# Local attention and a feed-forward network on one core: PE visits attention for two units at a time

## The chip, the core and the metric

The kernel runs on one core of a Trainium2 chip. It is one program; the metric is the device time of one execution in microseconds (us), as the median of three runs. Engines: PE (TensorE, the matrix unit, with PEld for its weight loads), ACT (ScalarE), DVE (VectorE), POOL (GpSimd) and SP, which here only issues DMAs. Every engine works through its own instructions in the order in which the program lists them; semaphores tie the engines together.

## The reference

Attention with 4 batches, 8 heads, 768 positions and 64 values per head, where a position sees the first 8 keys and the last 96 ones, with a slope per head; then a feed-forward network of 512 x 2048 over the 3072 tokens.

```python
scores = scale * np.matmul(q, k.transpose(0, 1, 3, 2))
keep = is_global | is_local              # first 8 keys; 0 <= i - j < 96
scores = np.where(keep, scores - slopes * dist, -1e9)
a = np.exp(scores - np.max(scores, axis=-1, keepdims=True))
a = a / (np.sum(a, axis=-1, keepdims=True) + 1e-09)
x = np.matmul(a, v)                      # as (3072, 512)
h = x @ w_in                             # (3072, 2048)
return np.maximum(0.01 * h, h) @ w_out   # (3072, 512)
```

## The kernel before

Both halves run in one stream on PE. The feed-forward half is cut into 8 chunks of 384 tokens and 16 slices f of the hidden 2048, which makes 128 steps j. A step is `ffn1(j)`, 12 matmuls of 384 columns into `ps_h` (H(j) below), and then `ffn2(j - 1)`, 9 matmuls of 512 columns into the three `ps_o` tiles of the chunk. Three matmuls stand where one would do in plain arithmetic, since x, the weights and the hidden values g are each split into a high and a low part (`xh`, `xl`, `wih`, `wil`, `gh`, `gl`). Between the two products stands `hidden`: ACT copies `ps_h` to t (L717), DVE takes the leaky maximum in place (L718), ACT rounds it to gh (L723), DVE takes the rest gl (L724). `ps_h` has one buffer, so H(j + 1) waits for the copy of H(j). PSUM is full: `ps_o` has 3 banks, `ps_h` one, and `ps_x` four, two under the tag `ps_av` and two under `ps_t`.

The attention half is cut into 48 units: 24 blocks of 128 queries (6 per batch), each with its 8 heads in two halves. A unit sees 192 gathered keys, in the first block of a batch (units 0, 1, 12, 13, 24, 25, 36, 37) 128. Unit u takes three visits of PE, called events: `event(t)` computes attention times v for unit t - 2 and the scores of unit t into the same two banks; all are 64x64 matmuls, four of which share the array. Units from 14 on (`BY_DVE`) are not transposed by PE: `sums` scales the probabilities by the reciprocal of their sum, DVE transposes 32x32 blocks (L232), and `move` writes them to DRAM (`via`) and reads them back into `pt`. The tag `ps_t` served the transposes of units 0 to 13 alone.

Behind the matmuls of an event the order in the code is: ACT copies x of unit t - 2 out of PSUM (`keep_x`, L313); POOL splits it into xh and xl (`split_x`, L43 and L326; x has one buffer); DVE adds the biases of unit t and takes the largest values (`biased`, four L188, which wait for the copy of x); ACT takes four exponentials with their sums (`exps`, L201); DVE forms rs (L222, L223), scales (four L229) and transposes. From step 23 on these instructions are not pinned to the order of the code (`pin`): the framework's scheduler sorts them among the steps' t, gh and gl, when the program is built.

`ev_at` tells at which step an event stands: the six events of a chunk were spread over 14 of its 16 steps, two or three apart. x of a chunk must be whole when the steps of that chunk begin.

Of the kernel before, what the change touches and what calls it, by code (L numbers as in the profile page):

```python
# [10 lines left out]
F32 = mybir.dt.float32  # L11
# [7 lines left out]
P = 128  # L19
D = 64  # L20
NU = 2
BY_DVE = 14
TB = 32
G = 32
# [9 lines left out]
def spread(items, slots):  # L34

    out = {}
    for n, x in enumerate(items):
        out.setdefault(slots[n * len(slots) // len(items)], []).append(x)
    return out
# [7 lines left out]
def fast_path(ctx, tc, qp, kp, vp, wi, wo, nvec, weights, nmall, out, B, H, S):  # L47
# [4 lines left out]
    NF = wi.shape[0]  # L52
# [14 lines left out]
    ps_x = ctx.enter_context(tc.tile_pool(name="ps_x", bufs=1, space=bass.MemoryType.PSUM))  # L67
# [42 lines left out]
    units = {}  # L110
    NUNIT = NSTEP * NU
    LEAD = NU * CHUNKS[0]

# [12 lines left out]
    def head(u, pr, a, j):  # L126

        if u < BY_DVE:
            n = 2 * j + a
# [11 lines left out]
    def load_qk(u):  # L141
        s, uu, i = where(u)
        if uu == 0:
            qs[s] = raw.tile([P, 2 * NU, P], F32, tag="qkr", name="qs")
            nc.sync.dma_start(out=qs[s], in_=qp[s])
        k = raw.tile([P, 2, 2, KW], F32, name="kr")
        if i:
            nc.sync.dma_start(out=k, in_=kp[s, uu])
        elif u < BY_DVE:
            nc.sync.dma_start(out=k[:, :, :, HALF:], in_=kp[s, uu][:, :, :, HALF:])  # L150
        else:
            kd, ks = (x.rearrange("p a f (s x) -> p (a f s) x", s=2) for x in (k, kp[s, uu]))
            nc.sync.dma_start(out=kd[:, :, TB:], in_=ks[:, :, TB:])
        units[u] = dict(q=qs[s][:, 2 * uu:2 * uu + 2], k=k)

    def load_v(u):
        s, uu, i = where(u)
        v = raw.tile([P, 5, 2, D], F32, name="vr", bufs=3)
        g0 = 0 if i else 3
        nc.sync.dma_start(out=v[:, g0:], in_=vp[s, uu][:, g0:])  # L160
        units[u]["v"] = v

    def scores(u, av):
        d = units[u]
        s, uu, i = where(u)
        q, k = d.pop("q"), d.pop("k")


        for a in range(2):
            for f in range(2):  # L170
                qf = slice(f * HALF, (f + 1) * HALF)
                for j in range(2):
                    rows = slice(j * D, (j + 1) * D)
                    tc.keep_in_program_order(nc.tensor.matmul(  # L174
                        own(u, av[qf, j, a * KW:(a + 1) * KW]), lhsT=q[rows, a, qf], rhs=own(u, k[rows, a, f, :]),
                        start=True, stop=True))

    def biased(u, ps):
        d = units[u]
        s, uu, i = where(u)  # L180
        pr = att.tile([P, 4 * KW], F32, name="pr")
        nm = nmall[:, 4 * u:4 * u + 4]
        for a in range(2):
            for j in range(2):
                nb = (nbw if i else nb0)[:, 4 * uu + 2 * a + j, :]
                if u >= BY_DVE:
                    nb = nb.rearrange("p (s x) -> p s x", s=2)
                pin(nc.vector.tensor_tensor_reduce(  # L188
                    out=head(u, pr, a, j), in0=own(u, ps[:, j, a * KW:(a + 1) * KW]), in1=nb, scale=-0.125, scalar=3.0e38,
                    op0=ALU.add, op1=ALU.min, accum_out=nm[:, 2 * a + j:2 * a + j + 1]))  # L190
        d.update(pr=pr, nm=nm)
# [92 lines left out]
    def attn_v(u, av):  # L284
        d = units[u]
        s, uu, i = where(u)
        v, pt = d["v"], d["pt"]

        def near(rows, j, g, f):

            if u < BY_DVE:
                return pt[rows, 3 * j + g] if f is None else pt[rows, 3 * j + g, f]
            n = g if where(u)[2] else g - 1
            return blocks(u, pt)[rows, slice(0, 4) if f is None else slice(2 * f, 2 * f + 2), j, n * TB:(n + 1) * TB]

        for j in range(2):
            for a in range(2):
                rows, out = slice(a * HALF, (a + 1) * HALF), slice(j * D, (j + 1) * D)
                tc.keep_in_program_order(nc.tensor.matmul(av[out, a, 2 * KW:], lhsT=v[rows, 4, j, :], rhs=near(rows, j, 2, None),  # L299
                                 start=True, stop=False))  # L300
        for f in range(0 if i else 1, 2):
            for g in range(0 if i else 1, 2):
                for j in range(2):
                    for a in range(2):
                        rows, out = slice(a * HALF, (a + 1) * HALF), slice(j * D, (j + 1) * D)
                        tc.keep_in_program_order(nc.tensor.matmul(av[out, a, 2 * KW + f * HALF:2 * KW + (f + 1) * HALF],  # L306
                                         lhsT=v[rows, 2 * f + g, j, :], rhs=near(rows, j, g, f),
                                         start=False, stop=(f == 1 and g == 1)))

    def keep_x(u, av):  # L310
        d = units[u]
        x = att.tile([P, 2, P], F32, name="x", bufs=1)
        pin(nc.scalar.copy(out=x, in_=av[:, :, 2 * KW:]))  # L313
        d["x"] = x

    def split_x(u):
        x = units.pop(u)["x"]
        s, uu, i = where(u)
        c = max(c for c in range(NCHUNK) if first_step[c] <= s)
        si = s - first_step[c]  # L320
        if c not in xt:
            xt[c] = [xts.tile([P, NK, CT], F32R, tag="xt", name=name) for name in ("xh", "xl")]
        cols = slice(si * P, (si + 1) * P)
        xh, xl = xt[c][0][:, 2 * uu:2 * uu + 2, cols], xt[c][1][:, 2 * uu:2 * uu + 2, cols]
        pin(copy_exact(nc.gpsimd, xh, x))
        pin(nc.gpsimd.tensor_tensor(out=xl, in0=x, in1=xh.bitcast(F32), op=ALU.subtract))  # L326

    def event(t, conv=()):

        now, mid, old = t < NUNIT, t - 1 in units, t - 2 in units  # L330
        if t < LEAD + 2:

            av = (ps_lead if t % 2 else ps_x).tile([P, 2, 512], F32, tag="ps_av", name="ps_sc")
            scores(t, av)
            if mid:
                transposes(t - 1)
            if old:
                ov = ps_lead.tile([P, 2, 512], F32, tag="ps_ov", name="ps_ov")
                attn_v(t - 2, ov)
        else:  # L340

            ov = av = ps_x.tile([P, 2, 512], F32, tag="ps_av", name="ps_av")
            attn_v(t - 2, ov)
            if now:
                scores(t, av)
            if mid:
                transposes(t - 1)
            keep_x(t - 2, ov)
        if t + 2 < NUNIT:
            load_qk(t + 2)  # L350
        if t + 1 < NUNIT:
            load_v(t + 1)
        if t < STAGES - 3:
            load_piece(t + 2)
        ends = due[:]
        due.clear()
        if ends:
            ends[0]()
        scale, shift, low = conversion(conv[0]) if conv else [lambda: None] * 3
        scale()  # L360
        if now:
            biased(t, av)
            exps(t)
        if ends:
            ends[1]()
        shift()
        if now:
            sums(t)
        low()
        if mid:  # L370
            keep_pt(t - 1)
        if old and t < LEAD + 2:
            keep_x(t - 2, ov)
        if old:
            split_x(t - 2)


    half = 7
    order = ([(0, f) for f in range(half)] + [(1, f) for f in range(NF)] + [(0, f) for f in range(half, NF)]
# [44 lines left out]
    for c in range(1, NCHUNK):  # L424
        events = range(NU * first_step[c] + 2, NU * first_step[c + 1] + 2)
        slots = (range(0, half - 1) if c == 1 else [23, 25, 26, 28, 29, 31] if c == 2 else [33, 35, 37, 40, 42, 44] if c == 3
                 else range((c - 1) * NF, c * NF - 2))
        ev_at.update(spread(events, slots))

    for t in range(2):  # L430
# [13 lines left out]
    for j in range(len(order) + 1):  # L444
        pinned[0] = j < half + NF
        conv = list(conv_at.get(j, ()))
        for t in ev_at.get(j, ()):
            event(t, conv[:1])
            conv = conv[1:]

        def end():
            for step in due:
                step()
            due.clear()

        def more():
            for n, p in enumerate(conv):
                if n:
                    end()
                for step in conversion(p):  # L460
                    step()
        if j == half:

            scale_bias(tc, tabs[:, 1], nbw, H, 2)
            scale_bias(tc, tabs[:, 0, HALF:], nb0, H, 2)
        if j < len(order):
            ffn1(j, end, more)
        if j:
            ffn2(j - 1)
# [342 lines left out]
```

## Time and profile before

| what | us |
|---|---|
| runs | 663.36, 663.47, 665.22 (median 663.47) |
| profiled execution, its own time | 663.89 |
| its span, first to last instruction | 662.0 |
| PE busy | 629.2 |
| DVE busy | 360.3 |
| ACT busy | 284.1 |
| POOL busy | 81.1 |

The span is what the profile's page divides; the execution's own time is 1.9 us longer. Busy times are unions of an engine's instructions. In the rows of the views below, a row is an engine, a line of the kernel, the operation, what it writes from what it reads, and how many; in the timeline it begins with the start and the length in us and ends, in brackets, with the engine's idle time before it and the instruction that ended it.

### The profile page before, as it was taken

Reading aid. Unit: us, or ns where it says so; the run is one execution under the profiler, and the core shown is the slowest. Engines: PE = TensorE matmul, PEld = TensorE weight load, DVE = VectorE, ACT = ScalarE, POOL = GpSimd, SP = SyncE. Lnnn points to the kernel's source line nnn. Section 1 sums busy time; section 2 is a strip of 40 time slices with the busy share of each in tenths; the row PEclk is TensorE's granted clock in tenths of the full one; section 3 lists DMA queues with packets and bytes.
Section 4 is the critical chain, followed back from the end, with each engine's and each line's share of the span. In section 5 each row is a group of like instructions: output and inputs, shape, how many; then the busy total and the mean of one; then the engine's idle time right before and its main releaser. Section 6 shows DMA issues by size and latency. Waiting matters only on the chain.

```text
span 662.0 us, 14799 instructions
## 1 busy us (share of the span) xinstructions
PE 629.2 (95%) x5803; PEld 552.0 (83%) x5803; DVE 360.3 (54%) x1073; ACT 284.1 (43%) x796; POOL 81.1 (12%) x146
## 2 busy tenths in 40 slices
PE   4669989999999999999999999999999999999994
PEld 3558879898888888888888888988888888999993
DVE  4968988887566545464544545355453644222221
ACT  5877755454444343353434343353342433232221
POOL 3344610000111010010100101010100011000000
PEclk9889999999999999999999999999999999999998
DMA  8785634332665543254441543245442431010001
GB/s 315 250 322 185 215 120 142 127 96 76 216 212 193 192 119 120 96 191 149 151 154 62 188 125 120 84 147 169 135 173 61 171 92 49 1 48 1 1 0 53
DMA packets 55166, 88.09 MB, mean 133 GB/s; under 512 B 9776, under 2 KB 30256, under 8 KB 55088
## 3 DMA queue, kind: packets, MB, share of 16 engines
q1 hardware_dynamic: 55088, 87.06, 39.9%
q8 instruction: 48, 0.79, 0.5%
q14 instruction: 30, 0.25, 0.1%
HBM read 67.90 MB, written 19.14 MB: 131 GB/s over the span
## 4 chain that ended last, share of the span: by engine, by line
PE 89%; DVE 3%; ACT 3%; DMA 2%; issue 1%; SPq 0%; POOL 0%; ACTq 0%; POOLq 0%; DVEq 0%
PE ps_h L713 14%; PE ps_h L714 13%; PE ps_h L715 13%; PE ps_o L736 13%; PE ps_o L734 13%; PE ps_o L735 13%; PE ps_av L174 4%; PE ps_av L306 3%; PE ps_av L299 2%; DMA kr<-in_kp_dram 2%; PE ps_tr L260 1%; ACT pr L201 1%; DVE w L489 1%; DVE w L493 1%; ACT w L484 0%
## 5 line engine op out<-in xcount | busy, mean ns | idle before, releaser
L713 PE MATMUL ps_h<-xh,wih 128*128 128x384 f32 x512 | 177.1, 346 | 0.0
L714 PE MATMUL ps_h<-xl,wih 128*128 128x384 f32 x512 | 172.3, 337 | 0.0
L715 PE MATMUL ps_h<-xh,wil 128*128 128x384 f32 x512 | 172.3, 336 | 0.0
L734 PE MATMUL ps_o<-woh,gh 128*128 128x512 f32 x384 | 150.2, 391 | 2.6 <-ACT kept L403 1.7
L736 PE MATMUL ps_o<-woh,gl 128*128 128x512 f32 x384 | 151.7, 395 | 0.1
L735 PE MATMUL ps_o<-wol,gh 128*128 128x512 f32 x384 | 150.5, 392 | 0.0
L718 DVE SCALAR_TENSOR_TENSOR t<-t 128x384 f32<-128x384 f32 x128 | 73.1, 571 | 137.8 <-ACT t L717 137.7
L717 ACT COPY t<-ps_h 128x384 f32<-128x384 f32 x128 | 60.6, 473 | 191.1 <-PE ps_h L715 191.1
L713 PEld LDWEIGHTS ps_h<-xh,wih 128*128 128x128 f32 x512 | 96.6, 189 | 13.4 <-issue 8.8
L714 PEld LDWEIGHTS ps_h<-xl,wih 128*128 128x128 f32 x512 | 96.6, 189 | 3.6
L715 PEld LDWEIGHTS ps_h<-xh,wil 128*128 128x128 f32 x512 | 96.5, 188 | 0.0
L724 DVE TENSOR_TENSOR gl<-t,gh 128x384 fp32r<-128x384 f32 x128 | 73.8, 576 | 40.6 <-ACT gh L723 40.6
L723 ACT CAST gh<-t 128x384 fp32r<-128x384 f32 x128 | 65.7, 513 | 66.8 <-DVE t L718 65.0
L201 ACT ACTIVATE pr<-pr,nmall 128x192 f32<-128x192 f32 (+1 forms) x192 | 83.4, 436 | 18.5 <-DVE nmall L188 18.0
L736 PEld LDWEIGHTS ps_o<-woh,gl 128*128 128x128 f32 x384 | 72.1, 188 | 16.8 <-DVE gl L724 1.6
L734 PEld LDWEIGHTS ps_o<-woh,gh 128*128 128x128 f32 x384 | 72.1, 188 | 14.4 <-ACT kept L403 2.1
L735 PEld LDWEIGHTS ps_o<-wol,gh 128*128 128x128 f32 x384 | 72.1, 188 | 11.1
L43 POOL TENSOR_SCALAR xh<-x 128x256 fp32r<-128x256 f32 x48 | 20.9, 435 | 435.4 <-ACT x L313 362.1
L188 DVE CUSTOM_DVE_ANT_0 pr<-ps_av,nbw 128x192 f32<-128x192 f32 x136 | 40.5, 354 | 52.5 <-ACT x L313 52.5
L313 ACT COPY x<-ps_av 128x256 f32<-128x256 f32 x42 | 15.6, 373 | 73.3 <-PE ps_av L174 69.4
L326 POOL TENSOR_TENSOR xl<-x,xh 128x256 fp32r<-128x256 f32 x48 | 37.0, 772 | 4.0
L201 ACT ACTIVATION_READ_ACCUMULATOR pr<-pr,nmall 128x1 f32 x192 | 36.2, 188 | 0.0
(84 smaller groups left out, 485.1 us busy)
## 6 DMA issues: line engine op xcount, KB each, us to landing
kr<-in_kp_dram SPq DMA_DIRECT2D x40, 384.0 KB, 3.9
vr<-in_vp_dram SPq DMA_DIRECT2D x40, 320.0 KB, 3.3
via<-pr SPq DMA_DIRECT2D x30, 384.0 KB, 2.3
pt<-via SPq DMA_DIRECT2D x120, 96.0 KB, 2.3
wst<-in_wi_dram SPq DMA_DIRECT2D x16, 512.0 KB, 3.6
wst<-in_wo_dram SPq DMA_DIRECT2D x16, 512.0 KB, 3.6
qs<-in_qp_dram SPq DMA_DIRECT2D x24, 256.0 KB, 4.2
out_dram<-part SPq DMA_DIRECT2D x21, 256.0 KB, 2.1
```

The costliest lines, as they stand in the source:

```text
L188: pin(nc.vector.tensor_tensor_reduce(out=head(u, pr, a, j), in0=own(u, ps[:, j, a * KW:(a + 1) * KW]), in1=nb, scale=-0.125, scalar=3.0e38 ...
L201: pin(nc.scalar.activation(out=p, in_=p, func=AF.Exp, scale=-1.0, bias=nm[:, 2 * a + j:2 * a + j + 1], accum_out=sm[:, 2 * a + j:2 * a + j ...
L713: tc.keep_in_program_order(nc.tensor.matmul(ps, lhsT=wih[:, k, fs], rhs=xh[:, k, :CT], start=(k == 0), stop=False))
L714: tc.keep_in_program_order(nc.tensor.matmul(ps, lhsT=wih[:, k, fs], rhs=xl[:, k, :CT], start=False, stop=False))
L715: tc.keep_in_program_order(nc.tensor.matmul(ps, lhsT=wil[:, k, fs], rhs=xh[:, k, :CT], start=False, stop=(k == NK - 1)))
L717: pin(nc.scalar.copy(out=t, in_=ps))
L718: pin(nc.vector.scalar_tensor_tensor(out=t, in0=t, scalar=0.01, in1=t, op0=ALU.mult, op1=ALU.max))
L723: pin(nc.scalar.copy(out=gh, in_=t))
L724: pin(nc.vector.tensor_tensor(out=gl, in0=t, in1=gh.bitcast(F32), op=ALU.subtract))
L734: tc.keep_in_program_order(nc.tensor.matmul(o, lhsT=gh[:, ts_], rhs=woh[:, f, :], start=first, stop=False))
L735: tc.keep_in_program_order(nc.tensor.matmul(o, lhsT=gh[:, ts_], rhs=wol[:, f, :], start=False, stop=False))
L736: tc.keep_in_program_order(nc.tensor.matmul(o, lhsT=gl[:, ts_], rhs=woh[:, f, :], start=False, stop=last))
```

## The change

From unit 22 on `event(t)` is replaced by `visit(t, t + 1)`. It computes attention times v for the units t - 2 and t - 1, then the scores of t and t + 1, each unit in two banks of its own: the even one under `ps_av`, the odd one under `ps_t`. Then come the copies and splits of both x, the biases and exponentials of both, and the sums, transposes and moves of both. A chunk has three visits, in its steps 1, 6 and 11, in place of six events; in the chunk before the change of pace the events 20 and 21 and the visits 22 and 24 stand at the steps 0, 3, 7 and 12 of it.

```diff
+PAIRS = 22
+    def visit(*ts):
+        for t in ts:
+            if t - 2 in units:
+                avs[t] = ps_x.tile([P, 2, 512], F32, tag="ps_t" if t % 2 else "ps_av", name="ps_v")
+                attn_v(t - 2, avs[t])
+        for t in ts:
+            if t < NUNIT:
+                scores(t, avs[t])
+        for t in ts:
+            if t + 2 < NUNIT:
+                load_qk(t + 2)
+            if t + 1 < NUNIT:
+                load_v(t + 1)
+        for t in ts:
+            keep_x(t - 2, avs[t])
+            split_x(t - 2)
+        for t in ts:
+            if t < NUNIT:
+                biased(t, avs.pop(t))
+                exps(t)
+        for t in ts:
+            if t < NUNIT:
+                sums(t)
...
+        if c > 3:
+            events, slots = events[::2], [(c - 1) * NF + s for s in (1, 6, 11)]
+        elif c == 3:
+            events, slots = [20, 21, 22, 24], [2 * NF + s for s in (0, 3, 7, 12)]
...
-            event(t, conv[:1])
+            if t >= PAIRS:
+                visit(t, t + 1)
+            else:
+                event(t, conv[:1])
```

How the built program stands on three engines (rows in the order of the program; x4 is four in a row). Lines of the changed file lie 1 to 36 further down. PE at the unit 30, before:

```order
L736 MATMUL ps_o<-woh,gl 128x512
L299 MATMUL ps_av<-pt,vr 64x128 x4
L306 MATMUL ps_av<-pt,vr 64x64 x16
L174 MATMUL ps_av<-kr,qs 64x192 x8
L713 MATMUL ps_h<-xh,wih 128x384
L714 MATMUL ps_h<-xl,wih 128x384
```

and now:

```order
L772 MATMUL ps_o<-woh,gl 128x512
L300 MATMUL ps_v<-pt,vr 64x128 x4
L307 MATMUL ps_v<-pt,vr 64x64 x16
L300 MATMUL ps_v<-pt,vr 64x128 x4
L307 MATMUL ps_v<-pt,vr 64x64 x16
L175 MATMUL ps_v<-kr,qs 64x192 x16
L749 MATMUL ps_h<-xh,wih 128x384
```

The matmuls of unit 31, which stood two steps later, now stand between the same two matmuls of the feed-forward half. ACT at the same place, before:

```order
L313 COPY x<-ps_av 128x256
L201 ACTIVATE pr,sm<-pr,nmall 128x2x96 x4
L717 COPY t<-ps_h 128x384
L723 CAST gh<-t 128x384
L717 COPY t<-ps_h 128x384
```

and now, at the visit of 28 (five steps earlier, the rows up to the second gh) and at that of 30:

```order
L314 COPY x<-ps_v 128x256
L202 ACTIVATE pr,sm<-pr,nmall 128x2x96 x4
L314 COPY x<-ps_v 128x256
L202 ACTIVATE pr,sm<-pr,nmall 128x2x96
L753 COPY t<-ps_h 128x384
L202 ACTIVATE pr,sm<-pr,nmall 128x2x96 x3
L759 CAST gh<-t 128x384
L753 COPY t<-ps_h 128x384
```

```order
L314 COPY x<-ps_v 128x256
L202 ACTIVATE pr,sm<-pr,nmall 128x2x96 x4
L314 COPY x<-ps_v 128x256
L202 ACTIVATE pr,sm<-pr,nmall 128x2x96 x4
L753 COPY t<-ps_h 128x384
L759 CAST gh<-t 128x384
```

The copy of ps_h behind a visit now stands behind five exponentials or behind eight. The first form is found at the visits of 22, 26, 28, 32, 38, 40 and 44, the second at those of 24, 30, 34, 36, 42 and 46. DVE at unit 30, before (biases of the unit ahead of these rows):

```order
L222 TENSOR_SCALAR rs<-sm 128x4
L223 RECIPROCAL rs<-rs 128x4
L718 SCALAR_TENSOR_TENSOR t<-t 128x384
L229 TENSOR_SCALAR pr<-pr,rs 128x2x96 x4
L724 TENSOR_TENSOR gl<-t,gh 128x384
L232 STREAM_TRANSPOSE pr<-pr 128x768
```

and now (biases of unit 30 ahead of them; of the four biases of unit 31 the first is shown):

```order
L223 TENSOR_SCALAR rs<-sm 128x4
L224 RECIPROCAL rs<-rs 128x4
L230 TENSOR_SCALAR pr<-pr,rs 128x2x96 x4
L189 ISA pr,nmall<-ps_v,nbw 128x2x96
...
L233 STREAM_TRANSPOSE pr<-pr 128x768
L223 TENSOR_SCALAR rs<-sm 128x4
L224 RECIPROCAL rs<-rs 128x4
L230 TENSOR_SCALAR pr<-pr,rs 128x2x96 x4
L754 SCALAR_TENSOR_TENSOR t<-t 128x384
L233 STREAM_TRANSPOSE pr<-pr 128x768
L760 TENSOR_TENSOR gl<-t,gh 128x384
```

The scales of unit 30 moved ahead of the biases of unit 31, and the step's t behind the scales of both. At the visits of the first form the four biases stand straight behind the first reciprocal, and the scales behind them; at those of 24 and 36 as well, but there t stands behind both transposes.

More of the change, by code (lines that the diff above doesn't have):

```diff
@@ L375, in event @@
             split_x(t - 2)
+    def visit(*ts):
[21 more added lines that the diff above has]
+                sums(t)
+    avs = {}
     half = 7
```

## The prediction

> **What bounds the kernel now.** I read the page's head first, then the busy time of PE (TensorE) over the stretch that the change touches (columns: stretch, length, busy time, matmuls, granted clock, DMA share, GB/s).
>
> ```profile
> span 662.0 us, 14799 instructions
> PE 629.2 (95%) x5803; PEld 552.0 (83%) x5803; DVE 360.3 (54%) x1073; ACT 284.1 (43%) x796; POOL 81.1 (12%) x146
> 235.00:560.00 325.00, 325.00 (x2784) 1.00 0.40 129
> ```
>
> From 235 to 560 us PE has work in flight all the time at the full granted clock: this stretch costs what PE's instructions cost, and PE waits for nobody. So two questions decide: what PE pays less, and whether the others still keep up. PE's timeline, one step without a visit and one behind a visit (start, length, then the group):
>
> ```profile
> 310.56 0.34 PE L713 MATMUL ps_h<-xh,wih 128*128 128x384 f32 x1
> ...
> 312.64 0.39 PE L734 MATMUL ps_o<-woh,gh 128*128 128x512 f32 x1
> ...
> 314.48 0.40 PE L736 MATMUL ps_o<-woh,gl 128*128 128x512 f32 x1
> 314.80 0.45 PE L299 MATMUL ps_av<-pt,vr 64*64 64x128 f32 x8
> 315.07 0.64 PE L306 MATMUL ps_av<-pt,vr 64*64 64x64 f32 x32
> 315.54 0.83 PE L174 MATMUL ps_av<-kr,qs 64*64 64x192 f32 x16
> 316.30 0.44 PE L713 MATMUL ps_h<-xh,wih 128*128 128x384 f32 x1
> 316.58 0.34 PE L714 MATMUL ps_h<-xl,wih 128*128 128x384 f32 x1
> ...
> 320.55 0.34 PE L713 MATMUL ps_h<-xh,wih 128*128 128x384 f32 x1
> ```
>
> Narrower windows show where the second group of four starts inside L299 and inside L174:
>
> ```profile
> 314.96 0.29 PE L299 MATMUL ps_av<-pt,vr 64*64 64x128 f32 x4
> 315.70 0.67 PE L174 MATMUL ps_av<-kr,qs 64*64 64x192 f32 x12
> ```
>
> A bare step is 12 matmuls H(j) into ps_h in 2.08 us (0.173 each) and 9 into ps_o in 2.07 (0.23 each): 4.15. Around the visit four things cost more than streaming: from L736 to L299 0.32 in place of 0.23; the first group of four L299 0.16 where the second takes 0.11; the last L174 group, 0.76 for four groups where one takes 0.16; the first L713 0.28 in place of 0.17. Together 0.09 + 0.05 + 0.11 + 0.10 = 0.35 us a visit: the price of going into 64x64 tiles and back. [...]
>
> **What ACT, DVE and POOL do behind such a visit:**
>
> ```profile
> 316.49 0.37 ACT L313 COPY x<-ps_av 128x256 f32<-128x256 f32 x1 [1.98 <-PE ps_av L174]
> 317.30 0.46 ACT L201 ACTIVATE pr<-pr,nmall 128x192 f32<-128x192 f32 x1 [0.43 <-DVE nmall L188]
> ...
> 319.07 0.45 ACT L717 COPY t<-ps_h 128x384 f32<-128x384 f32 x1
> 320.15 0.52 ACT L723 CAST gh<-t 128x384 fp32r<-128x384 f32 x1 [0.62 <-DVE t L718]
> ```
>
> ```profile
> 316.89 0.36 DVE L188 CUSTOM_DVE_ANT_0 pr<-ps_av,nbw 128x192 f32<-128x192 f32 x1 [1.79 <-ACT x L313]
> ...
> 318.01 0.08 DVE L188 DVE_READ_ACCUMULATOR2_ANT nmall<- 128x1 f32 x1
> 319.19 0.17 DVE L222 TENSOR_SCALAR rs<-sm 128x4 f32<-128x4 f32 x1 [1.10 <-ACT pr L201]
> ...
> 319.56 0.56 DVE L718 SCALAR_TENSOR_TENSOR t<-t 128x384 f32<-128x384 f32 x1
> 320.03 1.00 DVE L229 TENSOR_SCALAR pr<-pr,rs 128x192 f32<-128x192 f32 x4
> 320.94 0.56 DVE L724 TENSOR_TENSOR gl<-t,gh 128x384 fp32r<-128x384 f32 x1
> 321.41 0.97 DVE L232 STREAM_TRANSPOSE pr<-pr 128x768 f32<-128x768 f32 x1
> ```
>
> ```profile
> 316.95 0.41 POOL L43 TENSOR_SCALAR xh<-x 128x256 fp32r<-128x256 f32 x1 [12.88 <-ACT x L313]
> 317.44 0.74 POOL L326 TENSOR_TENSOR xl<-x,xh 128x256 fp32r<-128x256 f32 x1
> ```
>
> I count from the start of H(j) behind the visit, 316.30. The copy of ps_h, t(j), stands on ACT behind the four exponentials: 2.77 to 3.22. PE wants ps_h back at 4.25 (320.55; ps_h has one buffer): 1.03 us to spare. gh(j) ends at 4.37 and gl(j) at 5.20; the second product wants them at 4.25 + 2.08 = 6.33 and, its third matmul, at 6.79. This slack is the cover of the whole softmax, and a double visit puts twice the softmax in front of the same t(j).
>
> **The change, part by part.** Units 22 to 49 are 28 visits of one, and become 14 of two. PE's matmuls for them are the same, the second unit's follow in the same tiles. Gain: 14 x 0.35 = 4.9 us. Bounds: nothing, if the second unit starts as dearly as the first; 6.3, if its two L299 groups stream at the pace of L306 besides (0.47 for eight, 0.06 in place of 0.11: 0.10 less a visit). I take 4.9, since in the rows the dear start comes once, at the change of shape.
>
> The double visit on ACT: x(t), four exponentials, x(t+1), exponentials of t+1, and t(j) among or behind these. x(t) is free when the scores of t are done, which is 4 x 0.16 = 0.65 earlier against H(j): x(t) at 0.19 - 0.65 = -0.46, exponentials (0.81 later) 0.35 to 2.12 (319.07 - 317.30 = 1.77 for four), x(t+1) 2.12 to 2.49. POOL costs nothing here: it frees x 1.69 after x(t)'s start, at 1.23. DVE takes rs of t 0.12 after ACT's last exponential, at 2.24, and is free 0.37 later, 2.61. From here the two forms of the order part.
>
> *Biases of t+1 next (seven visits, beginning with units 22, 26, 28, 32, 38, 40, 44).* They start at 2.61, the first exponential 0.41 later at 3.02, then t(j) stands behind this one: 3.46 to 3.94. PE waits only past 4.2: spare 0.26, no stall. DVE: biases to 3.81, scales of t 0.91, t(j) 0.47, the transpose 0.95, rs 0.17, so gl(j) ends near 6.8 where it is wanted at 6.75: 0 to 0.2 us each; I take 0.06, together 0.4.
>
> *Scales of t first (units 30, 34, 42, 46).* Biases of t+1 start at 2.61 + 0.91 = 3.52, exponentials at 3.93, and t(j) stands behind all four: 5.70 to 6.18. What PE loses on top at a restart, an older wait shows:
>
> ```profile
> 166.59 0.58 ACT L416 COPY part<-ps_o 128x512 f32<-128x512 f32 x1
> ```
>
> ```profile
> 167.22 0.50 PE L734 MATMUL ps_o<-woh,gh 128*128 128x512 f32 x1 [0.65 <-ACT part L416]
> 167.55 0.39 PE L735 MATMUL ps_o<-wol,gh 128*128 128x512 f32 x1
> ```
>
> 0.05 after the copy's end, and 0.33 to the next matmul in place of 0.23: 0.10. So H(j+1) starts at 6.23 in place of 4.25: 1.98 + 0.10 = 2.1 us. Behind it rs of t+1 at 5.8, scales 6.2 to 7.1, t(j) to 7.7, gh(j) to 8.2 (wanted at 8.4), the transpose to 8.55, gl(j) to 9.05 (wanted at 8.85): 0.2 + 0.1. Sum 2.4 each, three times 7.2. In the visit of 46 the flag's seven small DVE instructions stand between as well:
>
> ```profile
> L585 DVE TENSOR_REDUCE fl<-nmall 128x1 f32<-128x192 f32 x1 | 0.4, 353 | 0.0
> ```
>
> They hold t(j) and gl(j) some 1.0 us longer (0.35 and six shorter ones): 3.3.
>
> *First blocks (units 24 and 36), whose scores have 128 columns:*
>
> ```profile
> 255.04 0.37 ACT L313 COPY x<-ps_av 128x256 f32<-128x256 f32 x1 [1.78 <-PE ps_av L174]
> 255.78 0.40 ACT L201 ACTIVATE pr<-pr,nmall 128x128 f32<-128x128 f32 x1 [0.37 <-DVE nmall L188]
> ...
> 257.35 0.46 ACT L717 COPY t<-ps_h 128x384 f32<-128x384 f32 x1
> ```
>
> ```profile
> 255.45 0.29 DVE L188 CUSTOM_DVE_ANT_0 pr<-ps_av,nb 128x128 f32<-128x128 f32 x1 [1.60 <-ACT x L313]
> ...
> 258.31 0.87 DVE L229 TENSOR_SCALAR pr<-pr,rs 128x128 f32<-128x128 f32 x4
> ...
> 259.56 0.71 DVE L232 STREAM_TRANSPOSE pr<-pr 128x512 f32<-128x512 f32 x1
> ```
>
> x(t) at 0.19 - 4 x 0.11 = -0.24; exponentials 0.50 to 2.07; biases of t+1 at 2.56, exponentials 2.89 to 4.46, t(j) to 4.94: H(j+1) at 4.99, 0.74 + 0.10. On DVE t(j) stands behind scales and transpose of both units, until about 6.7; gh(j) ends at 7.8, wanted at 7.15: 0.7 + 0.1. Sum 1.6 each, 3.2. The last visit, 48, has no scores and costs nothing.
>
> SP issues the same transfers; what is new is that the second unit's way through DRAM stands behind the first's four reads:
>
> ```profile
> 322.42 0.33 SPq L212 DMA_DIRECT2D via<-pr  x1
> pt<-via SPq DMA_DIRECT2D x120, 96.0 KB, 2.3
> ```
>
> First write near 6 (late form 9.9), reads 2.3 later for 1.8, second write and reads as long again, landing 2.3: near 17 (20.4). The next visit comes 5 or 6 steps on, at 20.8 at the earliest, and where the form is late PE is 2.4 later too. This costs nothing; with three steps it would.
>
> Sum: -4.9 + 0.4 + 7.2 + 3.3 + 3.2 = +9.2 us. The profiled execution took 663.89 us (span 662.0 and 1.9 around it), 0.42 above the median 663.47; from the first 673.1, from the median 672.7. I predict 672.7.
>
> **Rivals.** (1) *The switch alone counts*: the softmax stays covered, and only the drain goes: 663.5 - 4.9 = 658.6. It holds if t(j) ends by 4.2 in all visits; for it speak the 1.03 us to spare in the trace, against it that in six visits t(j) is queued behind all of the second unit's exponentials, which start at 2.9 to 3.9. [...] Chance 0.05. [...]
> (2) *x(t) is freed only with the scores of t+1*: everything on ACT and DVE is 0.65 (0.43 in first blocks) later: 4 x 0.65 + 2 x 0.43 = 3.5, and the seven good visits lose 0.39 + 0.1 at t(j) and 0.2 at gl(j), 4.8: 681. Against it: in the trace x waits for its own unit's L174. Chance 0.04.
> (3) *The clock falls after the stalls.* If a step behind each of the six ran at half speed: 6 x 4.15 = 25, 698. Against it:
>
> ```profile
> 92.00:96.00 4.00, 2.25 (x12) 1.00 0.29 93
> ```
>
> PE stood idle for 1.75 us there, and the granted clock stayed 1.00. Chance 0.02.
> (4) *Gain and stalls cancel*: the late forms cost 0.8 us each in place of 1.6 to 3.3. It needs PE's wait to be shorter than in-order queues make it. 0.04.
>
> **Numbers.** The forecast has 0.85. Its own range: the gain between 0 and 6.3, the good visits between 0 and 1.4, and 15% on the stalls of 13.7, not all at one end: 669.5 to 676.5; this holds just over eight in ten, and no rival lies in it. A measurement here tells about 0.3%, 2 us. Slower by more: 0.85 + 0.04 + 0.02 = 0.91; same 0.04; faster 0.05.
>
> **What the profile after would show.** Right: 14 visits of about 2.9 us; behind those of 24, 30, 34, 36, 42 and 46 L713 waits for "ACT t" (0.7 to 2.0 us), the others nothing; L734 or L736 wait for gh or gl 0.2 to 0.9 in the same places; the gap at the first L713 unchanged at 0.28. Wrong: no waits for t (rival 1), waits behind all visits (2), or a granted clock below 1.00 behind them (3). The forecast fails if the program's order on ACT and DVE isn't what decides when t(j) runs.

## The result, and the profile after

The changed kernel takes 678.94 us (median of four runs, 678.24 to 680.92) against 663.41 us (660.97 to 665.22) before: a ratio of 1.0235, interval 1.0205 to 1.0265. It is slower, as forecast, but by 15.5 us in place of 9.2, and outside the range of 669.5 to 676.5. The profiled execution took 680.92 us. Its head, and the same stretch as before (PE's busy time is the first figure behind the length; the granted clock stands third from the end):

```profile
span 679.1 us, 14768 instructions
PE 632.2 (93%) x5803; PEld 556.8 (82%) x5803; DVE 361.1 (53%) x1073; ACT 283.7 (42%) x796; POOL 81.4 (12%) x146
```

```profile
235.00:560.00 325.00, 315.29 (x2734) 278.78 (x2732) 153.49 (x509) 121.17 (x364) 30.28 (x52) 0.99 0.39 125
```

The stretch that PE filled without a gap has 9.7 us of idleness now, and the clock in it is no longer 1.00. The view of waits names who is waited for:

```profile
PE ps_h L749 <- ACT t L753: 10.3, 6, 2.4
PE ps_sc L175 <- DMA kr<-in_kp_dram: 10.1, 5, 5.1
...
PE ps_o L770 <- ACT gh L759: 1.8, 3, 0.8
```

Six waits for t, none longer than 2.4 us: they stand behind the visits of 24, 30, 34, 36, 42 and 46, the six that were forecast. The second row lies ahead of the first double visit, where both programs are the same; it was 6.9 us in the profile of before, and varies from run to run. PE's timeline of the visit of 30 and 31, then the step behind it:

```profile
338.66 0.67 PE L307 MATMUL ps_v<-pt,vr 64*64 64x64 f32 x32
339.12 1.51 PE L175 MATMUL ps_v<-kr,qs 64*64 64x192 f32 x32
340.56 0.44 PE L749 MATMUL ps_h<-xh,wih 128*128 128x384 f32 x1
340.84 0.34 PE L750 MATMUL ps_h<-xl,wih 128*128 128x384 f32 x1
...
344.64 0.39 PE L772 MATMUL ps_o<-woh,gl 128*128 128x512 f32 x1
347.37 0.44 PE L749 MATMUL ps_h<-xh,wih 128*128 128x384 f32 x1 [2.33 <-ACT t L753]
```

The way back to 128x128 costs 0.28 once (340.56 to 340.84) for two units; the whole visit takes 2.86 in place of two of 1.50. Then H(60) comes 6.81 behind H(59), where 4.25 was free of waiting. What held t(59), on ACT, DVE and POOL:

```profile
345.09 0.46 ACT L202 ACTIVATE pr<-pr,nmall 128x192 f32<-128x192 f32 x1 [2.08 <-DVE nmall L189]
...
346.86 0.46 ACT L753 COPY t<-ps_h 128x384 f32<-128x384 f32 x1
```

```profile
343.21 1.57 DVE L230 TENSOR_SCALAR pr<-pr,rs 128x192 f32<-128x192 f32 x4
344.70 0.34 DVE L189 CUSTOM_DVE_ANT_0 pr<-ps_v,nbw 128x192 f32<-128x192 f32 x1
...
347.40 1.01 DVE L230 TENSOR_SCALAR pr<-pr,rs 128x192 f32<-128x192 f32 x4
```

```profile
343.10 0.41 POOL L44 TENSOR_SCALAR xh<-x 128x256 fp32r<-128x256 f32 x1 [1.33 <-ACT x L314]
343.59 0.85 POOL L327 TENSOR_TENSOR xl<-x,xh 128x256 fp32r<-128x256 f32 x1
```

The order is the forecast one: scales of unit t, biases of t + 1, four exponentials, t(j). But the four scales take 1.57 us, while POOL splits x of the second unit; those of unit 31 take 1.01 at 347.40, where POOL is idle.

By terms, measured between the starts of H(20) and H(127) in the two profiles (a stall is the time from H(j) behind the visit to H(j + 2), less 4.25 + 4.15):

| term | forecast, us | measured, us |
|---|---|---|
| 14 changes of shape fewer | -4.9 | -4.9 |
| seven visits in the early order | +0.4 | no wait |
| visits of 30, 34, 42 | +7.2 | 3.0 + 3.0 + 4.2 = +10.3 |
| visit of 46 | +3.3 | +3.2 |
| visits of 24, 36 (first blocks) | +3.2 | 2.0 + 2.0 = +4.0 |
| pace of all other steps | 0 | +2.1 |
| sum | +9.2 | +14.7 |

Between the two profiled executions lie 17.0 us: 14.8 in that stretch (the rows of the table leave 0.1 of it open), 3.1 of the lead-in ahead of H(20), and 0.9 less at the end.

### The profile page after: what moved, and what is told of

Read it like the earlier page. It is cut to its first block, busy times and chain, and to the rows that moved or that the text cites. A ratio compares the mean times of both kernels' runs of the same rounds, so it can differ in the third digit from the quotient of the medians.

```text
span 679.1 us, 14768 instructions
## 1 busy us (share of the span) xinstructions
PE 632.2 (93%) x5803; PEld 556.8 (82%) x5803; DVE 361.1 (53%) x1073; ACT 283.7 (42%) x796; POOL 81.4 (12%) x146
## 4 chain that ended last, share of the span: by engine, by line
PE 80%; DVE 8%; ACT 5%; DMA 3%; issue 2%; SPq 0%; POOL 0%; ACTq 0%; DVEq 0%
PE ps_h L749 12%; PE ps_o L772 12%; PE ps_o L770 12%; PE ps_o L771 12%; PE ps_h L750 12%; PE ps_h L751 12%; ACT pr L202 3%; DMA kr<-in_kp_dram 3%; PE ps_v L175 2%; DVE pr L230 2%; PE ps_v L307 2%; PE ps_v L300 1%; PE ps_av L175 1%; DVE pr L189 1%; DVE pr L233 1%
## 5 line engine op out<-in xcount | busy, mean ns | idle before, releaser
L749 PE MATMUL ps_h<-xh,wih 128*128 128x384 f32 x512 | 177.1, 346 | 10.3 <-ACT t L753 10.3
L770 PE MATMUL ps_o<-woh,gh 128*128 128x512 f32 x384 | 151.8, 395 | 4.2 <-ACT gh L759 1.8
L189 DVE CUSTOM_DVE_ANT_0 pr<-ps_v,nbw 128x192 f32<-128x192 f32 x88 | 26.2, 352 | 24.9 <-ACT x L314 24.9
L230 DVE TENSOR_SCALAR pr<-pr,rs 128x192 f32<-128x192 f32 (+1 forms) x136 | 36.3, 329 | 0.6
```

Source lines behind the costliest of these rows:

```text
L230: pin(nc.vector.tensor_scalar(out=p, in0=p, scalar1=rs[:, n:n + 1], scalar2=1.0, op0=ALU.mult, op1=ALU.mult))
L749: tc.keep_in_program_order(nc.tensor.matmul(ps, lhsT=wih[:, k, fs], rhs=xh[:, k, :CT], start=(k == 0), stop=False))
L770: tc.keep_in_program_order(nc.tensor.matmul(o, lhsT=gh[:, ts_], rhs=woh[:, f, :], start=first, stop=False))
```

## The experiments

All kernels below keep the double visit from unit 22 on. They fix the order of all engines by hand from step 38 on: `sums` is cut into rs, scales and transpose, and each part is put ahead of t(j), between t(j) and gh(j) (`early`), or behind gl(j) (`late`); a second entry of either list waits for the next step. Lines of helpers have other numbers there: `ps_h` is L787 to L796, t L791 to L800, the scales L257. The edits are shown shortened, with lines joined and conditions left out: those of e2, e3 and e7 against e1, those of e4, e5 and e6 against e3.

**The double visit without a stall (e1_clear).** The second unit's biases go behind t(j), its exponentials and the scales and transposes of both units behind gl(j).

```diff
+    if b < NUNIT: biased(a, avs[a]); exps(a)
+    keep(b)
+    recip(a)
+    early.append(lambda: biased(b, avs[b]))
+    late.extend([lambda: (exps(b), scaled(a), turned(a), recip(b)),
+                 lambda: (scaled(b), turned(b))])
```

> From step 38 on the order on ACT, DVE and POOL is fixed by hand: at a double visit ACT copies x of both units and then ps_h (t) at once, and the second unit's exponentials and scales come behind gh and gl of that step. PE's order, the DMAs and the arithmetic are those of the changed kernel. Theory (the loss is where t stands on ACT and DVE): no wait of PE for t, gh or gl behind any visit, the whole gain of the 14 saved switches is left, 663.4 - 4.9 = 658.5 us, at most 2 us more if PE's pace between visits stays as uneven as it was (4.17 to 4.21 us a step in place of 4.15). Rival (a double visit costs PE time as such: two more PSUM banks in use, twice the softmax in one go): PE still waits, and the time stays above 665 us.

Measured: 660.50 us (657.53 to 663.55) against 663.03 (660.59 to 665.87) before, ratio 0.9966, interval 0.9948 to 0.9985. Its head and its stretch:

```profile
span 657.0 us, 14768 instructions
```

```profile
235.00:560.00 325.00, 325.00 (x2883) 291.16 (x2882) 161.95 (x539) 127.21 (x381) 34.73 (x55) 1.00 0.41 130
```

PE is busy throughout, at the full clock: no wait is left, so the stalls of the changed kernel come from the order on the other engines and not from the double visit itself. The time lies at the upper end of what was expected, 658.5 and at most 2 us more. The gain at the medians is 2.5 us and not 4.9; between H(20) and H(127) of the profiles it is 3.4. What is missing there can only be pace, which the last experiment comes back to.

**The early order in all visits (e2_form1).** t(j) stands behind five exponentials, as in the seven visits that cost nothing.

```diff
-    early.append(lambda: biased(b, avs[b]))
+    biased(b, avs[b]); exps(b, (0,)); scaled(a)
+    early.extend([lambda: (exps(b, (1, 2, 3)), turned(a), recip(b, (0,))),
+                  lambda: turned(b)])
+    late.append(lambda: (recip(b, (1,)), scaled(b)))
```

> All 13 visits with scores in the first form: t of the step stands behind one exponential of the second unit, the other three behind t. Theory: t ends 0.26 us before PE wants ps_h, gl of the step comes 0 to 0.2 us late: 659 to 661.5 us, no wait for t. Rival (0.26 us is no margin on the chip, since POOL and DVE get in each other's way there too): PE waits for t or gl behind most visits, 0.3 us and more each, 663 us or above.

Measured: 661.84 us (659.89 to 663.71), ratio 0.9978, interval 0.9963 to 0.9994; PE waits for gh 0.3 us in all. That is 0.3 above the expected 661.5 and below the rival's 663; one step, the second behind the visit of 46 with the flag, took 5.02 us in place of 4.17, since gh and gl came late there. So the order alone, with the same double visit, decides whether the change costs or gains, though the gains are small: 0.2 to 0.3% in e1 and e2.

**The late order in all visits (e3_form2), and with a shorter operation on POOL (e4_form2_short).** Both put the scales of t ahead of the biases of t + 1 in all 13 visits, as the changed kernel does in four; the second also writes zeros into xl, which leaves the low part of x out of the product.

```diff
+    recip(a); scaled(a)
+    biased(b, avs[b]); exps(b)
+    turned(a); recip(b); scaled(b)
+    early.append(lambda: turned(b))
```

```diff
-    pin(nc.gpsimd.tensor_tensor(out=xl, in0=x, in1=xh.bitcast(F32), op=ALU.subtract))
+    pin(nc.gpsimd.memset(xl.bitcast(F32), 0.0))        # units from 22 on
```

> All 13 visits with scores in the second form: DVE scales the first unit ahead of the second unit's biases, and t stands behind all eight exponentials. Theory: each costs what the four such visits of the changed kernel cost, 3.0 us (2.0 in the two first blocks, 3.5 in the visit with the flag): 663.4 - 4.9 + 10 x 3.0 + 3.5 + 2 x 2.0 = 696 us, and 1.7 us more for every window at half clock, of which 13 stalls may bring two or three: 696 to 702. Rival (the six late visits were slow for the place they stood at, not for their order): the visits that were good stay good, 685 us or less.

> As the run with all visits in the second form, but from unit 22 on POOL writes zeros into xl in place of subtracting (the low part of x is left out of the product). Theory of the port: the third scale of the first unit takes 0.79 us in place of 0.32 because POOL's subtraction (0.74 us, longer there) runs at the same time; without it the four scales take 0.9 us, and each of 13 visits is about 0.5 us shorter: 6 to 7 us below the run with the subtraction. Rival (DVE is slow there for a reason of its own): the same time within 2 us.

Measured: e3 706.87 us (706.27 to 708.67), ratio 1.066, interval 1.0635 to 1.0684; e4 699.32 us (698.85 to 701.77), ratio 1.0546, interval 1.052 to 1.0572. The expectation of e3, 696 to 702, was missed by 5 us. Its profile has six stretches at half the granted clock, explained below, where two or three had been reckoned with, and 1.8 us of pace between H(20) and H(127) that had been left out; together these make some 4 of the 5. The waits of e3, then of e4, and the scales of the same visit (30 and 31) with POOL's work beside them, again e3 and then e4; the second row of e3 is the third of the four scales, and the second row of e4 the first of them, each from a narrower window:

```profile
PE ps_h L793 <- ACT t L797: 29.5, 13, 2.4
```

```profile
PE ps_h L796 <- ACT t L800: 26.2, 13, 2.4
```

```profile
354.09 1.57 DVE L257 TENSOR_SCALAR pr<-pr,rs 128x192 f32<-128x192 f32 x4
354.64 0.79 DVE L257 TENSOR_SCALAR pr<-pr,rs 128x192 f32<-128x192 f32 x1
...
353.98 0.41 POOL L44 TENSOR_SCALAR xh<-x 128x256 fp32r<-128x256 f32 x1 [1.32 <-ACT x L338]
354.47 0.85 POOL L351 TENSOR_TENSOR xl<-x,xh 128x256 fp32r<-128x256 f32 x1
```

```profile
349.39 1.34 DVE L257 TENSOR_SCALAR pr<-pr,rs 128x192 f32<-128x192 f32 x4
349.39 0.66 DVE L257 TENSOR_SCALAR pr<-pr,rs 128x192 f32<-128x192 f32 x1
...
349.29 0.41 POOL L44 TENSOR_SCALAR xh<-x 128x256 fp32r<-128x256 f32 x1 [1.90 <-ACT x L338]
349.63 0.31 POOL L354 MEMSET xl<- 128x256 f32 x1
```

With POOL's second operation shorter, the same scales on DVE get shorter, and PE's 13 waits shrink by 3.3 us together: the length of DVE's scales does depend on what POOL does meanwhile. They don't reach the 1.01 us that they take alone, since e4's zeros still run beside them: the first scale takes 0.66 us and ends 0.11 behind POOL's L354. Of the 7.55 us between the medians only these 3.3, a quarter of a us a visit where half had been expected, are shown to come from it; another 2.1 us lie in the profiles' lead-ins, ahead of the first difference (H(20) at 145.27 and 143.13), and 1.2 behind H(127). So the near agreement with the expected 6 to 7 is luck.

Row by row, the third scale of e3 takes 0.79 us, where one beside an idle POOL takes 0.32 (the first of unit 31 in the changed kernel, at 347.40), and ends 0.11 behind POOL's L351. What holds it so long, a port as the expectation of e4 has it or something else, no run here shows.

**When does the clock fall?** In e3 some second steps behind a visit took 4.62 us and others 5.8, with a granted clock of 0.5 for 3.41 us (a slow stretch below); within one profile such stretches start only at whole multiples of 3.41 us from each other. Behind its visits the changed kernel has one, at the visit of 42. Three such stretches of it, one after the other (length, PE busy, and so on to the clock):

```profile
499.70:503.10 3.40, 3.40 (x19) 3.10 (x18) 2.23 (x11) 1.94 (x9) 1.96 (x3) 1.00 0.92 308
503.10:506.50 3.40, 1.03 (x6) 0.61 (x5) 3.13 (x16) 2.22 (x9) 0.00 (x0) 1.00 0.29 114
506.50:509.90 3.40, 3.40 (x12) 3.40 (x11) 2.33 (x6) 0.57 (x2) 0.00 (x0) 0.50 0.44 151
```

PE was idle for 2.37 us of the second, and the third runs at half the clock. Behind the visit of 30 the wait was as long (2.33), but a border of two stretches cut it:

```profile
342.64:346.05 3.41, 2.40 (x11) 1.65 (x9) 3.19 (x15) 1.33 (x8) 1.25 (x2) 1.00 0.76 268
346.06:349.46 3.40, 2.09 (x12) 2.03 (x12) 3.13 (x9) 1.77 (x7) 0.00 (x0) 1.00 0.30 119
```

Idle for 1.01 and 1.31, and the clock stayed. In e4 two waits lie on either side of the point; each pair is a stretch with the wait and the one behind it:

```profile
465.49:468.90 3.41, 1.53 (x9) 1.53 (x10) 3.13 (x13) 1.83 (x9) 0.00 (x0) 1.00 0.80 313
468.91:472.31 3.40, 3.40 (x11) 2.92 (x10) 2.20 (x4) 1.50 (x3) 0.00 (x0) 0.50 0.49 132
578.13:581.54 3.41, 1.56 (x7) 0.94 (x5) 3.41 (x17) 1.98 (x9) 0.83 (x4) 1.00 0.00 0
581.55:584.95 3.40, 2.99 (x15) 2.36 (x15) 3.40 (x15) 1.23 (x3) 0.00 (x0) 1.00 0.36 134
```

1.88 us of idleness in one stretch (3.41 less 1.53) came ahead of a halved clock in the next, 1.86 (3.41 less 1.56, unrounded) did not. This became a theory, and two kernels change the length of the wait: shorter in **e5_six**, where t(j) stands behind six exponentials, longer in **e6_long**, where the first transpose goes ahead of the second biases.

```diff
-    biased(b, avs[b]); exps(b)
-    turned(a); recip(b); scaled(b)
+    biased(b, avs[b]); exps(b, (0, 1))
+    turned(a)
+    early.extend([lambda: (exps(b, (2, 3)), recip(b)), lambda: turned(b)])
+    late.append(lambda: scaled(b))
```

```diff
     scaled(a)
+    turned(a)
     biased(b, avs[b]); exps(b)
-    turned(a)
```

> The late order in all 13 visits as in the run before (scales of t ahead of the biases of t + 1), but t(j) stands behind six exponentials, and the last two follow behind it. PE's wait at ps_h then is 0.70 us shorter, some 1.65 us in place of 2.35, and gl(j) no longer waits for the second unit's scales. Theory (the granted clock halves for 3.41 us where PE was idle for more than about 1.87 us of one of the fixed 3.41 us stretches before it): no half-clock record behind any of the 13 waits; 706.9 - 13 x 0.70 - 11 x 0.45 - 6 x 1.2 = 685.6 us. Rival (each stall has some chance of a slow stretch whatever its length): four to six such records, 691 us.

> The late order with the first unit's transpose too ahead of the biases of t + 1: everything behind it is 0.97 us later (0.70 in the two first blocks), so PE waits 3.3 us in 11 visits and 2.6 in two. Theory (more than about 1.87 us of idleness in one fixed 3.41 us stretch): a wait of 3.3 us misses this only where the border of two stretches cuts it nearly in half, which is 13% of the positions, and one of 2.6 us in 33%: 10 to 12 half-clock records in place of 6; 706.9 + 11 x 0.97 + 2 x 0.70 + 5 x 1.2 = 725 us. Rival (chance by the number of stalls, not their length): 6 records and 719 us.

Measured: e5 681.66 us (681.33 to 683.12), ratio 1.0284, interval 1.0243 to 1.0324; e6 728.1 us (723.96 to 731.38), ratio 1.0962, interval 1.0906 to 1.1017; before took 662.63 beside them (661.05 to 666.85). e5's waits and clock, then e6's waits and one of its visits in four stretches:

```profile
PE ps_h L792 <- ACT t L796: 18.6, 13, 1.5
```

```profile
240.00:560.00 320.00, 302.88 (x2606) 267.86 (x2599) 156.12 (x498) 118.08 (x358) 29.77 (x50) 1.00 0.40 127
```

```profile
PE ps_h L793 <- ACT t L797: 42.3, 13, 3.4
```

```profile
300.50:303.90 3.40, 1.39 (x7) 0.80 (x5) 3.27 (x13) 0.89 (x4) 0.85 (x1) 1.00 0.82 293
303.92:307.33 3.41, 2.04 (x6) 2.05 (x7) 2.35 (x8) 1.81 (x7) 0.00 (x0) 0.50 0.37 118
307.34:310.75 3.41, 3.41 (x11) 3.12 (x11) 1.35 (x3) 0.60 (x3) 0.00 (x0) 0.50 0.61 191
310.76:314.10 3.34, 3.34 (x19) 3.08 (x18) 0.56 (x1) 0.39 (x1) 0.00 (x0) 1.00 0.43 118
```

e5: no slow stretch behind 13 waits; e6: one behind each of 13, where 10 to 12 had been expected. The rival, a chance by the number of waits, falls. Behind the double visits of the changed kernel, e3, e4, e5 and e6 there are 60 waits, 58 for t and two for gh; in 26 the idle time within one stretch was 1.88 us or more, and all 26 were followed by a slow one; in 34 it was 1.86 or less, and none was.

The border is not as sharp as these 60 make it. Ahead of all visits, near 94 us, every kernel has one wait of 1.7 to 1.8 us behind the same matmuls of a step. It lies wholly within one stretch in e6 and in e1 (two rows each):

```profile
92.30:95.71 3.41, 1.64 (x8) 1.29 (x8) 2.66 (x6) 3.10 (x7) 0.00 (x0) 1.00 0.52 154
95.71:99.12 3.41, 3.41 (x12) 3.12 (x11) 3.13 (x6) 1.53 (x3) 0.00 (x0) 0.50 0.53 154
93.57:96.98 3.41, 1.64 (x8) 1.34 (x8) 2.66 (x6) 3.16 (x7) 0.00 (x0) 1.00 0.52 154
96.98:100.40 3.42, 3.42 (x20) 3.17 (x19) 3.14 (x7) 1.95 (x4) 0.00 (x0) 1.00 0.50 153
```

With 1.77 us of idleness both times the clock fell in e6, as it did in e2, and stayed in e1, as in the changed kernel (1.76). In the first 50 us, where PE works in short bursts of small matmuls, stretches with up to 1.99 us of idleness were not followed by a slow one (e6, from 24.03; in the kernel before 1.83, from 18.95). So in these profiles the idle time within one stretch decides in most places, but between some 1.75 and 2.0 us something else decides with it, which no run here shows.

Two sizes were off. The wait of e5 shrank by 0.88 and not 0.70 (two exponentials of 0.44), which is 2.3 of the 4 us that it came out below the expectation. e6 came out 3 us above its 725, which is within the 7 us over which its own runs spread; its profile also has what was not expected, that in five visits the slow stretch, itself idle for 0.7 to 1.4 us, was followed by a second one, for 1.1 us more each.

**The pace (e7_abab).** Without any wait, a bare step still takes 4.15 us in some places and up to 4.21 in others, at the full clock. The first matmuls of two steps in a row, in the changed kernel and at the same steps of e1:

```profile
483.60 0.34 PE L749 MATMUL ps_h<-xh,wih 128*128 128x384 f32 x1
...
487.82 0.34 PE L749 MATMUL ps_h<-xh,wih 128*128 128x384 f32 x1
```

```profile
465.70 0.34 PE L788 MATMUL ps_h<-xh,wih 128*128 128x384 f32 x1
...
469.85 0.34 PE L788 MATMUL ps_h<-xh,wih 128*128 128x384 f32 x1
```

The value is the same for all steps between two visits, and changes at a visit, with one exception: in e2 it went from 4.15 to 4.19 at step 61, with no visit near. Behind single visits it was 4.15 from step 26 to 104 of the kernel before; behind double ones it is 4.145, 4.167, 4.19 or 4.21. e7 is e1 with another order inside the visit.

```diff
     for t in ts:
         if t - 2 in units:
             attn_v(t - 2, avs[t])
-    for t in ts:
         if t < NUNIT:
             scores(t, avs[t])
```

> As the run without waits (660.5 us), but PE computes the values of t - 2, the scores of t, the values of t - 1, the scores of t + 1 in this order, so that the visit ends as two single visits would. If the pace of the bare steps behind a visit (4.145, 4.167 or 4.21 us) hangs on the order of the matmuls in it, all bare steps take 4.145, and 1.3 us go: 659.2. Rival: the pace is a matter of when the visit starts or how long it is, and stays mixed: 660.5. The tiles' shapes are the same in both orders; a second drain inside the visit would show as a visit of 3.0 us in place of 2.86.

Measured: 659.39 us (657.77 to 662.32), ratio 0.995, interval 0.9928 to 0.9971: the lowest median here, though its interval overlaps that of e1. But the expectation failed in its own terms: the pace was not 4.145 everywhere, it went to and fro, 4.167 and 4.145 behind one visit and the next. The value of 4.21, which e1 had behind one visit and the changed kernel behind three, did not appear, and a visit took 2.83 in place of 2.86. That explains 0.7 us in the profiles (329.97 in place of 330.63 from H(38) to H(108)); e1 and e7 ran beside different runs of before, so more can't be read from the medians. What sets the pace stays open.

## Why the prediction was wrong

- **The switch**: right. Two units in one visit save 0.35 us, and e1 and e2, almost without waits, come out 2.5 and 1.2 us below before, with intervals that leave out 1. The "drain" of rival (1) and of e7's expectation is the author's name for these 0.35 us: the rows show the dear starts at the change of shape, and no run shows what PE does there.
- **Which visits stall, and on what**: right, all six, each waiting for t on ACT behind the second unit's exponentials. Rival (1), the switch alone, failed; with the order of e1 it comes true, less the pace. Rival (2) failed: x(t) starts ahead of H(j), at 340.08 against 340.56.
- **The late form at 2.4 us**: mis-sized by 0.6 in each of the visits of 30, 34 and 42. The step that failed is "scales of t, 0.91", taken from a place where POOL was idle. In the double visit the second x is copied just before, and POOL's split of it falls on the scales. "POOL costs nothing here" was argued from when x comes free, not from what POOL does to DVE.
- **The clock**: the step that failed is the dismissal of rival (3) by one idle time of 1.75 us that left the clock at 1.00. That row was too near the border to settle it: at the same place 1.77 us in one stretch let the clock fall in e2 and e6. The forecast's own waits of 2.1 us lay above the 1.88 us from which, behind the visits, it always fell. It cost 1.2 us in the profiled execution, not the rival's 25: three of the four waits of 2.3 us and more were cut by a border of two stretches, with 1.01 and 1.31, 0.84 and 1.53, 1.04 and 1.33 us on its two sides, and left the clock at 1.00; the fourth, 2.37 us within one, was followed by one slow stretch of 3.41 us.
- **First blocks at 1.6 us**: mis-sized by 0.4 each. gh came 0.2 us later than reckoned, most of it again the scales (1.04 us for the four of unit 24 in place of 0.87, with POOL's split beside the first). Another 0.1 went at the third matmul of the second product, where PE waited for gl, which the sum left out.
- **The visit of 46**: 3.2 against 3.3, with two errors that cancel: the flag's instructions cost 0.2 in place of 0.9, the scales 0.6 more.
- **PE's matmuls "are the same"**: their number and shapes are, their pace is not. It cost 2.1 us over the other steps, where 0.4 had been set for gl.
- The range allowed 15% on the stalls; the stalls came out 28% larger, and the pace was no term at all. 1.8 (scales) - 0.1 (visit of 46) + 0.8 (first blocks) + 1.2 (clock) + 1.7 (pace) makes 5.4 of the 5.5 us that are missing between the two sums of the table. What sets the pace stays open.

## What to carry to other kernels

When two units of work are merged to save a fixed cost on one engine, first write out the queues of the others: here 4.9 us at the changes of shape were won, and six copies that had come to stand behind twice the softmax cost 17.5. Take a duration from a place where the same neighbours run; one taken beside an idle POOL was 0.6 us short. And a wait of PE was priced in two parts here: its own length, and, where 1.88 us or more of it lay within one stretch of 3.41 us of the clock's records, the slow stretch that followed; shortening e3's wait from 2.35 to 1.5 us brought 25 us at the medians, of which 13 waits by 0.88 are 11; most of the rest are the slow stretches and the waits for gl that went with them.

## What the runs showed of the hardware that was not expected

- Behind the double visits of the changed kernel and of e3 to e6 the granted clock fell to 0.5 for 3.41 us where PE had been idle for 1.88 us or more of the stretch of 3.41 us before (26 of 26), and not for 1.86 or less (0 of 34). Elsewhere it also fell after 1.77 (e2, e6) and did not after 1.99 (e6, small matmuls), so the value is no sharp limit. In the slow stretch the matmuls of H follow each other at 0.32 us in place of 0.176 (the changed kernel, from 506.72 and from 341.02). In e6, where the slow stretch itself was idle for 0.7 us or more, the next was slow as well (5 times); where it was idle for 0.56 or less, it was not.
- A scale of 128x192 on DVE that ran into POOL's subtraction took 0.79 us (e3) in place of 0.32, and POOL's took 0.85 in place of 0.74. Beside e4's writing of zeros a scale took 0.66; both ended 0.11 behind POOL's operation.
- The same 21 matmuls of a step take 4.145 to 4.21 us at the same granted clock, and but for one place (e2, step 61) the value changes only at a visit; what sets it is not known.
